# Attention block times SiLU of a GEGLU layer: output weights, last scalings, w_down pieces and first gate sums moved in the order

## The chip, the cores and the metric

The kernel runs on one core of one Trainium2 chip. The time is device microseconds (us) of one execution; the time of a kernel is the median over its runs. Engine names are those of the profile: PE is TensorE, PEld its weight loads, DVE VectorE, ACT ScalarE, POOL GpSimd, SP SyncE, which here only starts DMAs.

## The reference

```python
x  = A_x                                   # 1 x 2048 x 576
xn = layernorm(x)
qkv = xn @ wqkv                            # 32 heads of 18
p  = softmax(q k^T * 18**-0.5);  s = (p v, heads joined) @ wo
g  = silu((gelu_tanh(xn @ w_gate) * (xn @ w_up)) @ w_down)    # inner width 4608
out = x + s * g                            # float32
```

## The kernel before

**Arithmetic.** Products that need float32 accuracy are made of three matmuls: each operand is split into a high part (rounded copy) and a low part (value minus high part), and high x high, high x low and low x high are summed. The splits have names: `wh`, `wl` for the gate and up weights, `ah`, `al` for the GEGLU activations, `T` (both parts of w_down), `woh`, `wol` for the output weights, `oh`, `ol` for the attention result.

**Stages.** A first stage normalises x, transposes it and computes q, k, v into scratch in HBM. Then come 144 *sections*, n = 0 to 143. The tokens are cut into NF = 4 blocks b of 512, the inner width into 18 rounds r of two halves g, and a section multiplies one block by one 128-wide slice of w_gate and w_up: 27 pairs of matmuls, line 412. Its PSUM goes under the tag `f`, or at the end alternately `ring`, a ring of three buffers. Sections 11 to 138 carry the attention between their pairs: scores `pe`, maxima `pm`, values `acc`. Two sections make a *down product* down(b, r): seven products of 42 matmuls in all (line 523) in a Strassen-like scheme with seven accumulators M[0..6]. ScalarE copies them into M in the first round of a block (line 525), VectorE adds them later (line 527).

**Gate sums.** When a block is done, its M are combined into four quarters (`COMBINED`, line 544: four pairs p, q of in-place sums) and stored as `ys` (line 550, `QUARTERS` m = 6, 4, 1, 5). The next block's first down product overwrites M, so it waits for that. `combine_at(i, ...)` hooks a sum ahead of pair i of the next section; `gates` does it for the section after it. Block 0's sums are shared by VectorE (p) and GpSimd (q).

**The end.** The last five sections, 139 to 143, are made by `last_section`. Between them stand the last three down products, `last_down(0..2)`, and 16 output *steps*. `step` n projects 128 tokens (`project`, 28 matmuls, line 1032), multiplies by the gate and adds x (`multiply`), splits the attention result of step n + 2 and loads `ys` and x for later steps. Up to twelve of these stand before the last block's M is ready. `load_wo` and `split_wo` bring the output weights: ScalarE makes woh (line 993), GpSimd wol (line 995), in the buffers that later hold x and ys. The last two attention units (`rest`) are scaled by the reciprocals of their sums: `load_scale` (`on`, `od`), `scale` on GpSimd (lines 704 to 707), `store_scale` (13 small stores, lines 716 to 722). `load_scale` uses the same SBUF (`rawd`, `tsum`) that later holds more x (`xxs`). A down product reads w_down as four pieces of T, each a DMA from the scratch `ts` (`t_piece`, line 468).

**Order.** TensorE's order is written out. On the other compute engines a scheduler places instructions during the sections, within marked ones' program order; from the last five sections on, theirs is written out too. SyncE works through its DMAs in order: one that waits for a landing, for a free buffer or for data holds back all behind it.

Of the kernel before, what the change touches and what calls it, by code (L numbers as in the profile page):

```python
# [30 lines left out]
NU = NQ * NB  # L31
# [24 lines left out]
PIECES = ((0, 3, 7), (0, 0, 3), (1, 3, 7), (1, 0, 3))  # L56
# [25 lines left out]
def kernel(ctx: ExitStack, tc: tile.TileContext, x, wqkv, wo, w_gate, w_up, w_down, out):  # L82
    nc = tc.nc
# [84 lines left out]
    with tc.tile_pool(name="pro", bufs=1) as pro, tc.tile_pool(name="pps", bufs=1, space=PSUM) as pps:  # L168
# [34 lines left out]
        def load_x(b):  # L203
            keep = tc.keep_in_program_order if b == 1 else lambda i: i
            xr = []
            for j in range(4):
                xx = pro.tile([P, D + HR], F32, name="xx", bufs=4)
                keep(nc.sync.dma_start(xx[:, 0:D], x[b * TB + j * P:b * TB + (j + 1) * P, :]))
                xr.append(xx)
            return xr  # L210
# [254 lines left out]
    def t_piece(r, k, store=False):  # L465
        i, a, b = PIECES[k]
        t, d = f(FF["T"])[:, i, a:b].rearrange("p m d -> p (m d)"), ts[r][:, (7 * i + a) * DC:(7 * i + b) * DC]
        nc.sync.dma_start(*((d, t) if store else (t, d)))
# [45 lines left out]
    def down(b, r, then={}):  # L514
        if b == 0 and r < PLAIN:
            return down_plain()
        (ah, al), T, M = FF["A"], FF["T"], FF["M"]
        for m, (i, k) in PRODUCTS:
            py = ring("py")
            for t in range(2):  # L520
                tt = slice(t * P, (t + 1) * P)
                for n, (h, w) in enumerate(((ah, 0), (ah, 1), (al, 0))):
                    nc.tensor.matmul(py[:, t, 0:DC], h[:, i, tt], T[:, w, k], start=n == 0, stop=n == 2)  # L523
            if r == 0:
                nc.scalar.activation(M[:, m], py[:, :, 0:DC], AF.Copy)
            else:
                nc.vector.tensor_tensor(M[:, m], py[:, :, 0:DC], M[:, m], op=ALU.add)  # L527
            for eng, to, op, by in then.get(m, ()):
                eng.tensor_tensor(M[:, to], M[:, to], M[:, by], op=op)
        if r == NR - 1 and b < NB - 1:  # L530
            FF["gates"].append(b)
            if b == 0:
                combine_at(14, nc.vector, *COMBINED[0])
            else:
                for k in range(4):
                    combine_at(6 * k + 6, nc.gpsimd, *COMBINED[k])

    def combine_at(i, eng, p, q):
        FF["hooks"].setdefault(i, []).append(lambda: (combine(eng, *p), combine(nc.gpsimd, *q)))

    def combine(eng, to, op, by):

        M = FF["M"]
        tc.keep_in_program_order(eng.tensor_tensor(M[:, to], M[:, to], M[:, by], op=op))

    def store_gates(b):

        for i, c, m in QUARTERS:
            rows = slice(b * TB + TH * i, b * TB + TH * i + TH)
            nc.sync.dma_start(ys[rows, DC * c:DC * c + DC].rearrange("(t p) d -> p t d", p=P), FF["M"][:, m])  # L550

    def gates():

        for b in FF["gates"]:
            if b == 0:
                for i, k in ((2, 1), (8, 2), (13, 3)):
                    combine_at(i, nc.vector, *COMBINED[k])
                FF["hooks"].setdefault(20, []).append(lambda b=b: store_gates(b))
            else:
                store_gates(b)  # L560
        FF["gates"] = []
# [139 lines left out]
    def scale(u, i):  # L701

        o, d = (t[:, i, 0:TB] for t in SC)
        nc.gpsimd.tensor_tensor(o, o, d, op=ALU.mult)
        if u % NQ == NQ - 1:
            nc.gpsimd.tensor_scalar(d.bitcast(F32R), o, split_rows, 1.0, op0=ALU.mult, op1=ALU.mult)
            nc.gpsimd.tensor_tensor(o, o, d, op=SUB)

    def store_scale(u, i):

        j, g = divmod(u, NQ)
        o, d = (t[:, i, 0:TB] for t in SC)
        for a in range(QD):
            row, p = (QD * g + a) * DH, 32 * a + 1
            if row + DH <= R0:
                nc.sync.dma_start(on[j][row:row + DH, :], o[p:p + DH])
                continue
            k = max(0, R0 - row)
            if k:
                nc.sync.dma_start(on[j][row:R0, :], o[p:p + k])  # L720
            for t, to in ((d, row + k), (o, row + k + HR)):
                nc.sync.dma_start(on[j][to:to + DH - k, :], t[p + k:p + DH])
# [248 lines left out]
    with tc.tile_pool(name="epi", bufs=1, reuse_waits="tile") as epi:  # L971
# [2 lines left out]
        YY = [epi.tile([P, D], F32, name=f"yy{i}") for i in range(4)]  # L974
        OP = {}
        groups = [(b, j) for b in range(NB) for j in range(TB // P)]
        rest, pieces = list(range(scaled, NU)), []
        pool, vec, act = nc.gpsimd, nc.vector, nc.scalar
        n = 0

# [2 lines left out]
        def load_wo():  # L983
            for i, t in enumerate(RAW[:KT]):
                nc.sync.dma_start(t, wo[i * P:(i + 1) * P, :])
            for a in range(2):
                nc.sync.dma_start(RAW[KT][HR * a:HR * a + HR], wo[R0:D, :])
# [13 lines left out]
        def load_y(k):  # L1001
            if k < len(groups) and groups[k][0] < NB - 1:
                nc.sync.dma_start(YY[k % len(YY)], ys[rows(k), :])
# [5 lines left out]
        def split_o(k):  # L1009
            if k < len(groups):  # L1010
                b, j = groups[k]
                oh, ol = OP[k] = [epi.tile([P, KT, P], F32R, name=m, bufs=c) for m, c in (("oh", 3), ("ol", 2))]
                raw = f(KA)[:, OTS[b]:OTS[b] + KT, j * P:(j + 1) * P]
                act.activation(oh, raw, AF.Copy)
                vec.tensor_tensor(ol, raw, f(oh), op=SUB)
# [33 lines left out]
        def step():  # L1049
            nonlocal n  # L1050
            po = project(n)
            multiply(n, po)
            split_o(n + 2)
            b, j = groups[n]
            if b < 2 and j == TB // P - 1:
                load_o(b + 2)
            for t in pieces[:2]:
                t()
            del pieces[:2]
            load_y(n + len(YY))  # L1060
            load_x(n + len(XX))
            n += 1

        def load_raw(n):
            FF["raw"][n] = load_gu(n % (NR * G))

        def last_section(tag):

            n = FF["n"]
            FF["n"] += 1  # L1070
            g = n % G
            pairs, pg, pu = gate_up(tag)
            hooks, FF["hooks"] = FF["hooks"], {}
            nxt = FF["raw"].pop(n + 1, None)
            if nxt:
                split_gu(nxt, 0)
                split_gu(nxt, 1)
            for t in spread(pairs, (), 1, hooks):
                t()
            if nxt:  # L1080
                split_gu(nxt, 2)
            FF["w"] = nxt
            h = ffn.tile([P, 3 + 3 * g, TH], F32, name=f"h{g}", bufs=2 - g)
            t1 = h[:, 0:2].rearrange("p a t -> p (a t)")

            def gelu():
                act.activation(t1, pg, AF.Square)
                vec.scalar_tensor_tensor(t1, t1, 1.0 / GC, pg, op0=ADD, op1=ALU.mult)
                act.activation(t1, t1, AF.Tanh, scale=GC * GS)
                vec.scalar_tensor_tensor(t1, t1, 1.0, pg, op0=ADD, op1=ALU.mult)  # L1090
                vec.tensor_tensor(t1, t1, pu, op=ALU.mult)

            return h, gelu

        def last_down(k, then={}):
            r = NR - 3 + k
            down(NB - 1, r, then)
            if r + 1 < NR:
                pieces.extend(lambda i=i: t_piece(r + 1, i) for i in range(len(PIECES)))

        ctx.enter_context(tc.manual_schedule(engines={mybir.EngineType.Activation, mybir.EngineType.DVE, mybir.EngineType.Pool}))
        FF["down"].clear()
        first = FF["n"]
        load_raw(first + 2)
        h, gelu = last_section("f")
        todo.pop("rec")[0]()
        for i, u in enumerate(rest):
            load_scale(u, i)
        load_wo()
        for k in range(2):  # L1110
            load_y(k)
        load_raw(first + 3)
        gelu()
        sums_a(1, h, vec)
# [1 line left out]
        split_o(0)  # L1116
        h, gelu = last_section("ring")
        gelu()
        for i, u in enumerate(rest):
            scale(u, i)  # L1120
            store_scale(u, i)
        h1, gelu = last_section("f")
        last_down(0)
        split_wo()
        for k in range(3):
            load_x(k)
        for k in range(2, 4):
            load_y(k)
        split_o(1)
        gelu()  # L1130
        sums_a(0, h, pool)
        cut_a(0, h, pool, pool)
        sums_a(1, h1, pool)
        cut_a(1, h1, pool, pool)
        load_raw(first + 4)
        for m in ("rawd", "tsum"):
            t = ffn.tile([P, 2, D], F32, name="xxs", tag=m)
            XX.extend((t[:, 0], t[:, 1]))
        for t in pieces:
            t()  # L1140
        del pieces[:]
        for k in range(3, len(XX)):
            load_x(k)
        for k in range(3):
            step()
# [57 lines left out]
```

## Time and profile before

| | us |
|---|---|
| median of 3 runs | 2601.88 (2599.99 to 2603.06) |
| profiled execution, its own time | 2600.66 |
| its span, first to last instruction | 2598.9 |
| PE busy | 2553.1 (98% of the span) |
| DVE busy | 2083.8 (80%) |
| POOL busy | 1642.1 (63%) |
| ACT busy | 1465.4 (56%) |

The granted clock of TensorE was 0.994 on the mean. Times in a row of the profile count from the span's start. A wait is put down to the event that ended it.

### The profile page before, as it was taken

To read this page: it belongs to the slowest core of one execution; us is meant where nothing else is said; L and a number is where in the kernel's file an instruction comes from. 1 tells how busy PE (TensorE), PEld (TensorE's weight loads), DVE (VectorE), ACT (ScalarE), POOL (GpSimd) and SP (SyncE) were. 2 spreads that over 40 slices of the span, in tenths; PEclk is the share of its full clock that TensorE was granted. 3 is DMA by queue.
4 is the path that set the end of the run, shared out by engine and by line. 5 is a ranking of instruction groups with operands and counts; after the bars stand their busy time and mean duration, and the time that the engine had idled before them with its cause. 6 is when DMAs were issued, how large, how long until landed. Compare 5 with 4: busy or idle time off the path is not lost.

```text
span 2598.9 us, 52905 instructions
## 1 busy us (share of the span) xinstructions
PE 2553.1 (98%) x20548; PEld 1846.2 (71%) x20548; DVE 2083.8 (80%) x2360; ACT 1465.4 (56%) x1772; POOL 1642.1 (63%) x1710
## 2 busy tenths in 40 slices
PE   9999999999999999999999999999999999999987
PEld 8887766666666776666666667766666777667777
DVE  5325888888887888888887988888887988886455
ACT  3224366666666655555566666656566665566511
POOL 3105588888888856666667666666657666666661
PEclk9999999999999999999999999999999999999988
DMA  8855455555575566666786676666677666665673
GB/s 262 270 181 138 108 166 156 165 161 161 166 211 149 165 159 158 167 165 161 172 196 181 168 166 165 166 169 170 169 172 206 169 166 166 154 173 151 186 218 132
DMA packets 410465, 447.47 MB, mean 172 GB/s; under 512 B 107108, under 2 KB 286820, under 8 KB 410216
## 3 DMA queue, kind: packets, MB, share of 16 engines
q1 hardware_dynamic: 410216, 444.09, 64.6%
q8 instruction: 164, 2.69, 0.4%
q14 instruction: 85, 0.70, 0.1%
HBM read 347.59 MB, written 96.38 MB: 171 GB/s over the span
## 4 chain that ended last, share of the span: by engine, by line
PE 92%; POOL 2%; DMA 2%; DVE 1%; issue 1%; ACT 1%; SPq 0%; POOLq 0%; DVEq 0%; ACTq 0%
PE pg L412 21%; PE acc L874 17%; PE py L523 14%; PE pu L412 11%; PE pe L857 9%; PE pm L805 9%; PE po L189 7%; PE po L1032 2%; PE py L510 1%; DMA raw<-in_B_w_up_dram 1%; DVE mx L807 0%; DMA od<-rT 0%; PE pt L250 0%; DMA T<-ts 0%; POOL wl L112 0%
## 5 line engine op out<-in xcount | busy, mean ns | idle before, releaser
L858 ACT ACTIVATE pT<-pe 128x1024 f32<-128x1024 f32 x1024 | 1047.2, 1027 | 577.9 <-PE pe L857 544.6
L807 DVE TENSOR_REDUCE mx<-pm 128x2 f32<-128x1024 f32 x1024 | 1221.3, 1224 | 181.8 <-PE pm L805 165.7
L412 PE MATMUL pg<-xd,wh 64*128 64x512 f32 x2538 | 925.5, 396 | 1.9 <-ACT t L425 1.9
L412 PE MATMUL pu<-xd,wh 64*128 64x512 f32 x2538 | 925.7, 396 | 1.6 <-DVE t L426 1.6
L412 PEld LDWEIGHTS pg<-xd,wh 64*128 64x128 f32 x2538 | 467.9, 184 | 114.8 <-issue 56.9
L412 PE MATMUL pg<-xd,wl 64*128 64x512 f32 x1269 | 496.1, 391 | 1.1 <-POOL wl L117 1.1
L412 PE MATMUL pu<-xd,wl 64*128 64x512 f32 x1269 | 496.0, 391 | 0.0
L412 PEld LDWEIGHTS pu<-xd,wh 64*128 64x128 f32 x2538 | 468.2, 184 | 27.6 <-DVE t L426 2.9
L874 PE MATMUL acc<-pT,VS 128*32 128x512 f32 x4096 | 466.0, 595 | 0.0
L110 POOL TENSOR_SCALAR wh<-raw 128x384 fp32r<-128x384 f32 x402 | 215.5, 539 | 385.1 <-PE pu L412 262.7
L112 POOL TENSOR_TENSOR wl<-raw,wh 128x384 fp32r<-128x384 f32 x402 | 416.9, 1039 | 27.7
L805 PE MATMUL pm<-KA,QT 64*128 64x512 f32 x2048 | 414.1, 394 | 4.6 <-ACT pT L858 2.8
L857 PE MATMUL pe<-QT,KA 64*128 64x512 f32 x2048 | 411.2, 392 | 3.4 <-DVE mx L807 2.4
L523 PE MATMUL py<-T,ah 128*128 128x288 f32 x1876 | 385.0, 301 | 13.2 <-DMA T<-ts 9.9
L527 DVE TENSOR_TENSOR M<-py,M 128x576 f32<-128x576 f32 x448 | 339.0, 757 | 42.5 <-PE py L523 28.8
L523 PEld LDWEIGHTS py<-T,ah 128*128 128x128 f32 x1876 | 302.0, 190 | 68.0 <-issue 54.0
L441 POOL TENSOR_TENSOR al<-h,ah 128x512 fp32r<-128x512 f32 (+1 forms) x143 | 296.7, 2075 | 65.4 <-ACT ah L438 53.8
L874 PEld LDWEIGHTS acc<-pT,VS 128*32 128x32 f32 x4096 | 120.2, 110 | 276.6 <-issue 229.6
L523 PE MATMUL py<-T,al 128*128 128x288 f32 x938 | 277.8, 296 | 0.0
L857 PEld LDWEIGHTS pe<-QT,KA 64*128 64x128 f32 x2048 | 193.1, 184 | 115.0 <-DVE mx L807 28.6
L412 PEld LDWEIGHTS pg<-xd,wl 64*128 64x128 f32 x1269 | 234.1, 184 | 32.8 <-POOL wl L117 2.0
L412 PEld LDWEIGHTS pu<-xd,wl 64*128 64x128 f32 x1269 | 234.1, 184 | 13.2
(169 smaller groups left out, 2921.3 us busy)
## 6 DMA issues: line engine op xcount, KB each, us to landing
T<-ts SPq DMA_DIRECT2D x98, 576.0 KB
KA<-qk SPq DMA_DIRECT2D x768, 72.0 KB
T<-ts SPq DMA_DIRECT2D x98, 432.0 KB
raw<-in_B_w_gate_dram SPq DMA_DIRECT2D x144, 288.0 KB
raw<-in_B_w_up_dram SPq DMA_DIRECT2D x144, 288.0 KB
ts<-T SPq DMA_DIRECT2D x36, 576.0 KB
VS<-vs SPq DMA_DIRECT2D x128, 152.0 KB
qk<-t SPq DMA_DIRECT2D x72, 256.0 KB
```

The costliest lines, as they stand in the source:

```text
L110: first = nc.gpsimd.tensor_scalar(hi, raw, 1.0, 1.0, op0=ALU.mult, op1=ALU.mult)
L112: keep(nc.gpsimd.tensor_tensor(lo, raw, f(hi), op=ALU.subtract))
L189: nc.tensor.matmul(o, st, m, start=(i == 0), stop=(i == len(terms) - 1))
L412: nc.tensor.matmul(o, w[1 + wp][k][rr, c, :], xd[k][xp][rr, c, :], start=(i == 0), stop=(i == len(terms) - 1))
L441: keep(two.tensor_tensor(lo, raw, f(hi), op=ALU.subtract))
L523: nc.tensor.matmul(py[:, t, 0:DC], h[:, i, tt], T[:, w, k], start=n == 0, stop=n == 2)
L527: nc.vector.tensor_tensor(M[:, m], py[:, :, 0:DC], M[:, m], op=ALU.add)
L805: nc.tensor.matmul(pm[:, a], QS[u, r][rr, t * P:(t + 1) * P], KS[(u * NA + c) % KB][r][rr, :], start=True, stop=True)
L807: return nc.vector.tensor_reduce(MX[u][:, 2 * r:2 * r + 2, t, c], pm, axis=AX.X, op=ALU.max)
L857: nc.tensor.matmul(pe[:, a], KS[(u * NA + c) % KB][r][rr, t * P:(t + 1) * P], QS[u, r][rr, :], start=True, stop=True)
L858: nc.scalar.activation(PT[u, kt][:, 2 * r:2 * r + 2, :], pe, AF.Exp, scale=SCALE)
L874: nc.tensor.matmul(ACC[u][32 * a:32 * a + 32, :], VS[(u * NA + c) % VB][:, v:v + 32], pt[:, a, :], start=first, stop=last, skip_group_chec ...
```

## The change

There are four edits.

1. *Gate sums.* GpSimd's halves q of block 0's sums are hooked at pairs 6, 12, 18 and 24 of the section right behind the block, all four there; VectorE's first half p stays at pair 14 and its others at 2, 8 and 13 of the section behind that. The quarters m = 1 and 5 are stored at the end of the first of these sections, 4 and 6 at pair 19 of the second. Before, only the first q was in the first section, and all four stores came at pair 20. For blocks 1 and 2 only the order of p and q within a pair is swapped.
2. *Output weights.* `load_wo` stands ahead of section 139 in place of behind `load_scale`; `split_wo`, three x loads and two ys loads stand behind section 140 in place of behind section 141 and down(0).
3. *Last units.* `scale` stands behind section 141 and down(0), `store_scale` behind the load of the last raw weights. Before, both were behind section 140.
4. *w_down.* `last_down` issues its four T pieces at once. Before, the steps behind it issued two each, or they stood behind the load of the last raw weights. x is loaded one step less ahead.

```diff
@@ down, combine_at, store_gates, gates
+            for k, (p, q) in enumerate(COMBINED):
+                combine_at(6 * k + 6, nc.gpsimd, q)
+                if b > 0:
+                    combine_at(6 * k + 6, nc.gpsimd, p)
             if b == 0:
-                combine_at(14, nc.vector, *COMBINED[0])
-            else:
-                for k in range(4):
-                    combine_at(6 * k + 6, nc.gpsimd, *COMBINED[k])
+                combine_at(14, nc.vector, COMBINED[0][0])
...
-    def combine_at(i, eng, p, q):
-        FF["hooks"].setdefault(i, []).append(lambda: (combine(eng, *p), combine(nc.gpsimd, *q)))
+    def combine_at(i, eng, what):
+        FF["hooks"].setdefault(i, []).append(lambda: combine(eng, *what))
...
-    def store_gates(b):
+    def store_gates(b, some=range(7)):
         for i, c, m in QUARTERS:
+            if m not in some:
+                continue
...
             if b == 0:
+                store_gates(b, (1, 5))
                 for i, k in ((2, 1), (8, 2), (13, 3)):
-                    combine_at(i, nc.vector, *COMBINED[k])
-                FF["hooks"].setdefault(20, []).append(lambda b=b: store_gates(b))
+                    combine_at(i, nc.vector, COMBINED[k][0])
+                FF["hooks"].setdefault(19, []).append(lambda b=b: store_gates(b, (4, 6)))
@@ step
-            for t in pieces[:2]:
-                t()
-            del pieces[:2]
             load_y(n + len(YY))
-            load_x(n + len(XX))
+            load_x(n + len(XX) - 1)
@@ last_down
             if r + 1 < NR:
-                pieces.extend(lambda i=i: t_piece(r + 1, i) for i in range(len(PIECES)))
+                for i in range(len(PIECES)):
+                    t_piece(r + 1, i)
@@ the end
         load_raw(first + 2)
+        load_wo()
         h, gelu = last_section("f")
         todo.pop("rec")[0]()
+        for k in range(2):
+            load_y(k)
         for i, u in enumerate(rest):
             load_scale(u, i)
-        load_wo()
-        for k in range(2):
-            load_y(k)
...
         gelu()
-        for i, u in enumerate(rest):
-            scale(u, i)
-            store_scale(u, i)
-        h1, gelu = last_section("f")
-        last_down(0)
         split_wo()
         for k in range(3):
             load_x(k)
         for k in range(2, 4):
             load_y(k)
+        h1, gelu = last_section("f")
+        last_down(0)
         split_o(1)
         gelu()
+        for i, u in enumerate(rest):
+            scale(u, i)
...
         load_raw(first + 4)
+        for i, u in enumerate(rest):
+            store_scale(u, i)
...
-        for t in pieces:
-            t()
-        del pieces[:]
-        for k in range(3, len(XX)):
+        for k in range(3, len(XX) - 1):
             load_x(k)
```

GpSimd before, from the last low part of section 141's weights to the first sum of section 140's activations (`on`, `od` are the last units, `wh`, `wl` the weights of section 142):

```order
L112 TENSOR_TENSOR wl<-raw,wh 128x384
L704 TENSOR_TENSOR on<-on,od 128x512 x2
L706 TENSOR_SCALAR od<-on,split_rows 128x512
L707 TENSOR_TENSOR on<-on,od 128x512
L110 TENSOR_SCALAR wh<-raw 128x384
L112 TENSOR_TENSOR wl<-raw,wh 128x384
L110 TENSOR_SCALAR wh<-raw 128x384
L112 TENSOR_TENSOR wl<-raw,wh 128x384
L110 TENSOR_SCALAR wh<-raw 128x384
L112 TENSOR_TENSOR wl<-raw,wh 128x384
L991 MEMSET wol 64x576
L995 TENSOR_TENSOR wol<-xx_31043,woh 128x576
```

GpSimd now, from the same place (line numbers are four higher):

```order
L112 TENSOR_TENSOR wl<-raw,wh 128x384
L995 MEMSET wol 64x576
L999 TENSOR_TENSOR wol<-xx_31043,woh 128x576
L999 TENSOR_TENSOR wol<-xx_31044,woh 128x576
L999 TENSOR_TENSOR wol<-xx_31045,woh 128x576
L999 TENSOR_TENSOR wol<-yy_31048,woh 128x576
L999 TENSOR_TENSOR wol<-yy_31049,woh 64x576
L110 TENSOR_SCALAR wh<-raw 128x384
L112 TENSOR_TENSOR wl<-raw,wh 128x384
L110 TENSOR_SCALAR wh<-raw 128x384
L112 TENSOR_TENSOR wl<-raw,wh 128x384
L110 TENSOR_SCALAR wh<-raw 128x384
```

The five wol have gone from behind the scaling and the splits of section 142 to ahead of both; the scaling now follows these splits.

SyncE now, from the last piece of T for down(1) over the raw weights of section 143 to ys for step 4 (`on_72` is the last block's scaled result in HBM):

```order
L468 DMA T<-ts 128x864
L130 DMA raw<-in_B_w_gate_dram 64x9x128
L130 DMA raw<-in_B_w_up_dram 64x9x128
L720 DMA on_72<-on 18x512 x4
L724 DMA on_72<-on 8x512
...
L726 DMA on_72<-od 18x512
L726 DMA on_72<-on 18x512
L1011 DMA xxs<-in_A_x_dram 128x576 x3
L1051 DMA out_dram<-xx_31043 128x576
L1007 DMA yy_31046<-ys 128x576
```

The stores of the scaled units, which stood ahead of the x loads of the first steps, now stand behind the raw weights of section 143 and ahead of the loads into their own buffers (`xxs`), the first output and ys for step 4.

ScalarE behind down(1,0), before and then now (`M<-py` are the copies of the seven products, `T` the next w_down, `pT` the attention's exponentials):

```order
L525 ACTIVATE M<-py 128x576 x6
L483 ACTIVATE T<-tsum 128x1152
L525 ACTIVATE M<-py 128x576
L485 ACTIVATE T<-tsum 128x288
L486 ACTIVATE T<-rawd 128x576
L858 ACTIVATE pT<-pe 128x1024 x8
```

```order
L525 ACTIVATE M<-py 128x576 x5
L483 ACTIVATE T<-tsum 128x1152
L485 ACTIVATE T<-tsum 128x288
L486 ACTIVATE T<-rawd 128x576
L862 ACTIVATE pT<-pe 128x1024
L525 ACTIVATE M<-py 128x576 x2
L862 ACTIVATE pT<-pe 128x1024 x7
```

Two of the seven copies have moved behind the three T copies and the first pT.

More of the change, by code (lines that the diff above doesn't have):

```diff
@@ L976 @@
         groups = [(b, j) for b in range(NB) for j in range(TB // P)]
-        rest, pieces = list(range(scaled, NU)), []
+        rest = list(range(scaled, NU))
         pool, vec, act = nc.gpsimd, nc.vector, nc.scalar
```

## The prediction

> **What bounds the kernel now.** I read the page first, then the waits of the end, then TensorE's own rows there, then the engines and transfers that it waited for. The page:
>
> ```profile
> PE 2553.1 (98%) x20548; PEld 1846.2 (71%) x20548; DVE 2083.8 (80%) x2360; ACT 1465.4 (56%) x1772; POOL 1642.1 (63%) x1710
> PE   9999999999999999999999999999999999999987
> ```
>
> TensorE is full in every slice but the last two, so a change is worth what it takes out of TensorE's gaps. The waits from 2440 us to 2600 us name the gaps of the end (total, times, longest):
>
> ```profile
> PE po L1032 <- POOL wol L995: 10.5, 5, 9.4
> PE py L523 <- DMA T<-ts: 9.9, 2, 9.0
> ```
>
> TensorE's rows around them (start, duration; the wait ahead in brackets), first of the output step 0, then of the last down product:
>
> ```profile
> 2480.25 0.29 PE L1032 MATMUL po<-woh,oh 128*128 128x288 f32 x1
> 2489.94 0.61 PE L1032 MATMUL po<-wol,oh 128*128 128x288 f32 x1 [9.39 <-POOL wol L995]
> 2498.67 0.42 PE L1032 MATMUL po<-woh,KA 128*128 128x288 f32 x1
> 2498.91 0.32 PE L1032 MATMUL po<-wol,KA 128*128 128x288 f32 x1
> 2499.06 0.29 PE L1032 MATMUL po<-woh,oh 128*128 128x288 f32 x1
> 2548.57 0.37 PE L523 MATMUL py<-T,ah 128*128 128x288 f32 x1 [0.89 <-DMA T<-ts]
> 2557.91 0.61 PE L523 MATMUL py<-T,ah 128*128 128x288 f32 x1 [8.97 <-DMA T<-ts]
> 2566.06 0.30 PE L1032 MATMUL po<-woh,oh 128*128 128x288 f32 x1
> ```
>
> After each gap the matmuls start 0.24 us apart (2498.67 to 2498.91), later about 0.135. A gap therefore costs its length and a stretch at half rate. What the same work takes without a gap stands in the chain of waits (start, length):
>
> ```profile
> 2450.26 5.79 PE py L523 x42
> 2506.76 6.37 PE pgu L412 x54
> 2513.13 11.32 PE po L1032 x84
> 2549.51 8.36 DMA T<-ts
> ```
>
> Three steps of 28 matmuls take 11.32 us, so one takes 3.77 and one matmul 0.135. Step 0 took 2499.06 - 2480.25 = 18.81 us, so 15.0 are lost. The last down product waited 0.89 + 8.97 = 9.9 us and then ran from 2557.91 to 2566.06, 8.15 us against 5.79, so 2.4 more are lost. The end holds 15.0 + 9.9 + 2.4 = 27.3 us that no work needs.
>
> **The output weights ahead of the first stall.** GpSimd's rows show why wol was late (in brackets the idle time before):
>
> ```profile
> 2465.13 1.02 POOL L112 TENSOR_TENSOR wl<-raw,wh 128x384 fp32r<-128x384 f32 x1
> 2473.92 1.29 POOL L704 TENSOR_TENSOR on<-on,od 128x512 f32<-128x512 f32 x1 [2.56 <-DMA od<-rT]
> 2483.09 0.51 POOL L110 TENSOR_SCALAR wh<-raw 128x384 fp32r<-128x384 f32 x1 [5.68 <-DMA on<-on]
> 2486.79 0.99 POOL L112 TENSOR_TENSOR wl<-raw,wh 128x384 fp32r<-128x384 f32 x1
> 2488.49 4.11 POOL L995 TENSOR_TENSOR wol<-xx,woh 128x576 fp32r<-128x576 f32 x3
> 2492.56 2.77 POOL L995 TENSOR_TENSOR wol<-yy,woh 128x576 fp32r<-128x576 f32 x2
> 2495.29 0.72 POOL L447 TENSOR_TENSOR h<-h 128x256 f32<-128x256 f32 x1
> 2502.55 3.28 POOL L441 TENSOR_TENSOR al<-h,ah 128x1280 fp32r<-128x1280 f32 x1
> ```
>
> The five wol stood behind the scaling, which waited for od, and behind the splits of section 142, which began only at 2483.09. After the change they stand behind the splits of 141 alone, which end at 2466.15. They then wait only for ScalarE's woh:
>
> ```profile
> 2472.54 0.63 ACT L1089 ACTIVATE h<-h 128x512 f32<-128x512 f32 x1 [2.84 <-DVE h L1088]
> 2474.73 2.14 ACT L993 ACTIVATE woh<-xx 128x576 fp32r<-128x576 f32 x3 [1.56 <-DMA xx<-in_A_wo_dram]
> ```
>
> On SyncE's queue the wo loads now stand ahead of three T pieces, the store of the reciprocals and the scale loads, so the 1.56 us that woh waited for them should go, and woh follows the gelu at 2473.2 at 0.71 us a piece. The first wol can start at 2473.9 and five at 1.38 us end near 2480.8. Step 0 needs the first wol at 2480.4 and the fifth some 1.5 us later. The cover is thin, 1 us, but it is there: I take the whole 15.0, and each us that woh comes later costs under one.
>
> The Trainium skill, "TensorE: Matmul & The Clock Gate", Part 1, says that an idle TensorE drops to half clock and comes back after about 3.4 us of sustained work. In the last down product the half rate lasted longer: 2.4 us lost at 0.24 - 0.135 a matmul are 23 matmuls or 5.5 us. By the skill's window it would be an estimated 14 matmuls, 1.5 us lost for 2.4, and the sum 26.4; the measured row decides.
>
> **What is late next.** Everything behind step 0 comes 15.0 us sooner: section 142 at 2491.8, down(1) at 2509.5, down(2) at 2532.5. GpSimd: wol to 2480.8, the three splits of 142 (4.7 us from 2483.09 to 2487.78) to 2485.5, the scaling (three products of 1.29 us and a shorter one, 4.6 as an estimate) to 2490.1, sums and cuts of 140 and 141 (2495.29 to 2505.83, 10.5) to 2500.7. Section 142 needs its splits at 2491.8 and down(1) its cuts at 2509.5: 6 and 9 us of room, so both moves cost nothing unless the raw weights of 142 land over 6 us later than that. Scaling goes behind these splits and no more waits for od in front of them.
>
> **w_down asked for at once.** Before, two pieces of T went out per output step and the last pair only at 2549.51, landing 8.36 us later. Now all four follow down(1), which ends near 2515.3, in one group; at the same 8.4 us, doubled because four go together, they land by 2532 at the latest against a need at 2532.5. All 9.9 and 2.4 us go. Room: 0 to 8 us.
>
> **The price: the stores of the scaled units.** These 13 small stores stood from 2476 us on SyncE's queue; now they stand after the scaling and ahead of the x loads into the same buffers (xxs), the first outputs and ys for steps 4 and 5:
>
> ```profile
> 2476.22 2.07 SPq L716 DMA_DIRECT2D on<-on  x4
> 2484.69 0.33 SPq L722 DMA_DIRECT2D on<-on  x1
> ```
>
> They took 2476.22 to 2485.0, 8.8 us, of SyncE's time. From 2490.1 on that ends at 2498.9; three xxs loads, an output and the ys of step 4 follow, landing near 2505. VectorE needs it at the end of step 4, 2491.8 + 6.4 + 7.5 = 2505.7. The trace of before has no such wait, so I bound it: 0 if they land in time, 5 us if od lands twice the 2.56 us late that it cost before, and the scaling and its stores with it. I take 1.5. For the load of the last scaled units ahead of step 10, behind an output on the queue, I take 0.5. The x loads, one step less ahead, still have six steps of 3.77 us, which costs nothing. End: 27.3 - 2.0 = 25.3 us.
>
> **The gate sums of the first block.** They stood in the section ahead of down(1,0), and the copies of the next products into M waited:
>
> ```profile
> 788.87 1.40 POOL L544 TENSOR_TENSOR M<-M 128x576 f32<-128x576 f32 x1
> 790.30 0.65 ACT L525 ACTIVATE M<-py 128x576 f32<-128x576 f32 x1 [3.49 <-POOL M L544]
> 785.01 0.53 PE L523 MATMUL py<-T,ah 128*128 128x288 f32 x2
> 791.01 0.53 PE L523 MATMUL py<-T,ah 128*128 128x288 f32 x2 [2.57 <-ACT M L525]
> 795.61 0.33 PE L523 MATMUL py<-T,al 128*128 128x288 f32 x1
> 796.53 1.16 ACT L483 ACTIVATE T<-tsum 128x1152 fp32r<-128x1152 f32 x1
> 799.02 2.85 ACT L858 ACTIVATE pT<-pe 128x1024 f32<-128x1024 f32 x3
> 768.90 1.28 POOL L450 TENSOR_TENSOR h<-h,h 128x512 f32<-128x512 f32 x1 [2.78 <-DVE h L429]
> ```
>
> TensorE took 795.74 - 785.01 = 10.7 us for 5.79, so 4.9 are lost. Three GpSimd sums of 1.4 us, 4.3 in all, move one section up, into its idle 2.78; the cuts there end 1.5 us later, still ahead of down(1,0) at 785.01, where no wait for them shows. New is ScalarE's order behind down(1,0): the copies of two of the seven products come after the T copies (1.16, two shorter ones) and one pT (2.85 / 3 = 0.95), about 3.3 us, and hold two of three PSUM buffers for that time. That new wait lies between 0 and 3.3; most of it meets a TensorE that needs buffers for scores, so I take 2.4. Gain 4.9 - 2.4 = 2.5, bounds 0 to 4.9, and -1 if the maxima behind slip too.
>
> **Sum.** The profiled execution took 2600.66 us (span 2598.9): 2600.66 - 25.3 - 2.5 = 2572.9. The median of the three runs is 2601.88, 1.2 above that one, so the forecast is 2574. Alone it spans 2567 (27.3 and 4.9 gained, and the 3 us by which the runs differ) to 2580 (stores 5 us late, gate sums worth nothing).
>
> **Rivals.** *Transfers bound the end.* The queue of 2453 to 2558 us, then stretches of it (TensorE, its loads, VectorE, ScalarE, GpSimd, clock, share, GB/s):
>
> ```profile
> q1 hardware_dynamic: 13078, 23.45, 74.0%
> 2477.00:2480.00 3.00, 3.00 (x25) 3.00 (x24) 2.82 (x5) 2.38 (x4) 0.40 (x1) 1.00 1.12 195
> 2480.00:2492.00 12.00, 2.34 (x11) 1.75 (x9) 3.75 (x6) 1.15 (x2) 8.53 (x10) 0.72 0.25 66
> 2501.00:2510.00 9.00, 9.00 (x71) 8.16 (x71) 7.80 (x7) 1.26 (x2) 8.83 (x5) 1.00 1.03 385
> ```
>
> These 23.45 MB kept the engines busy for 0.74 x 105 = 77.7 us. They must now land by about 2541, in 88 us, a share of 0.88. The gaps to fill are there (0.25 from 2480 to 2492), but SyncE asks in order and may stand before a wait while they are empty. At a share of 0.80 the last lands at 2453 + 97 = 2550, 9 us late: 2583. At the old 0.74 it is 2558, 17 late: 2591. For it speaks the thin row of the stores, against it that T now stands early in the queue. Chance 0.22. The Trainium skill, "DMA: Bandwidth & Descriptors", Specifications, gives about 358 GB/s as a core's limit at HBM; by that the 23.45 MB would take an estimated 66 us and fit with ease. The trace has 385 in one stretch, above it, and 302 on average while busy, so the rows are the stricter measure, and I follow them.
>
> *The gate sums return their gain.* ScalarE's late copies push scores and maxima by the full 3.3 us and more: 2574 + 2.5 to 5, about 2577. Chance 0.08.
>
> *It does not do what it says.* woh comes late, say behind a wo load that waits for its buffers, and half of the first stall stays: 2574 + 7.5 = 2581.5. Against it, xx and yy are fresh buffers then. Chance 0.04.
>
> *Slower.* The packed transfers run at the rate that raw weights, od and wo ran at together, 195 GB/s at full share (the row at 2477). 23.45 MB then take 120 us and the last lands at 2573, 15 us after today's 2557.9: with the half-rate product back and the gate gain, 2600.66 + 15 - 2.5 + 1.2 = 2614. It decides for slower below 23.45 MB / 107 us = 219 GB/s. Against it stands 385 GB/s in the row at 2501, and 302 on average. Chance 0.06.
>
> **How the numbers follow.** The forecast has 0.60. From 2567 to 2587 the range holds it, the gate rival, the half stall and the milder half of the transfers, about 0.83. The measurement can tell 0.2%, 5 us: every case but the last lies over 8 us below 2601.88. Of the last's 0.06, 0.02 lies about no change; of the rest, 0.02 lies as near to either side. So faster 0.92, same 0.03, slower 0.05.
>
> **What would show it.** Right: wol at about 2474 to 2481 on GpSimd, no wait of po for wol, T of the last product in one group near 2515, its wait gone, down(2) done near 2540, and the tail of 2598.9 - 2566.06 = 32.8 us unchanged; around 785 no wait of M for GpSimd, and a new one for pT or M. Wrong: waits of VectorE for yy<-ys before down(1), of TensorE for T or KA near 2530 to 2545, or wol still behind od.

## The result and the profile after

The changed kernel takes 2575.94 us (median of 4 runs, 2575.34 to 2577.57), the kernel before 2601.89 us (4 runs); the ratio is 0.9902, 95% interval 0.9885 to 0.9919. Forecast were 2574 us, between 2567 and 2587. The profiled execution has a span of 2573.6 us, 25.3 less than before. The page of the changed kernel; TensorE is now full in 39 slices of 40:

```profile
PE 2546.1 (99%) x20548; PEld 1838.3 (71%) x20548; DVE 2089.8 (81%) x2360; ACT 1464.9 (57%) x1772; POOL 1640.2 (64%) x1710
PE   9999999999999999999999999999999999999998
```

TensorE's waits of the end, 2440 us to 2600 us. Both of before are gone (10.5 for wol, 9.9 for T). The wait of 1.6 for `ol` was there before; what has come is 1.4 for VectorE's multiply `yy` and short ones:

```profile
PE po L1036 <- DVE ol L1019: 1.9, 2, 1.6
PE py L523 <- DVE yy L1045: 1.4, 1, 1.4
PE py L523 <- DVE M L527: 0.8, 2, 0.5
```

GpSimd at the end: wol at 2472.18 to 2479.18, then a wait for the raw weights of section 142, the scaling, and the cuts to 2504.77:

```profile
2472.18 4.22 POOL L999 TENSOR_TENSOR wol<-xx,woh 128x576 fp32r<-128x576 f32 x3 [6.01 <-issue]
2476.37 2.81 POOL L999 TENSOR_TENSOR wol<-yy,woh 128x576 fp32r<-128x576 f32 x2
2483.32 0.52 POOL L110 TENSOR_SCALAR wh<-raw 128x384 fp32r<-128x384 f32 x1 [4.14 <-DMA raw<-in_B_w_up_dram]
2488.87 3.00 POOL L708 TENSOR_TENSOR on<-on,od 128x512 f32<-128x512 f32 x2
2501.82 2.95 POOL L441 TENSOR_TENSOR al<-h,ah 128x1280 fp32r<-128x1280 f32 x1
```

SyncE: ys for step 4 leaves at 2501.37, behind the 13 stores; T for the last down product in one group at 2525.18. TensorE takes that product up at 2534.36 without a wait and ends it at 2540.75:

```profile
2497.83 0.32 SPq L726 DMA_DIRECT2D on<-on  x1
2499.54 1.31 SPq L1011 DMA_DIRECT2D xxs<-in_A_x_dram  x3
2501.37 0.43 SPq L1007 DMA_DIRECT2D yy<-ys  x1
2525.18 1.81 SPq L468 DMA_DIRECT2D T<-ts  x4
```

The gate sums, 755 us to 812 us. TensorE's waits there are these; those of M for GpSimd (3.3 us of TensorE's time before) are gone, the maxima's are not:

```profile
PE pe L861 <- DVE mx L811: 3.7, 4, 1.9
PE pm L809 <- ACT pT L862: 2.1, 1, 2.1
PE pe L861 <- ACT M L525: 0.3, 1, 0.3
```

Before, the waits for the maxima in the same stretch were these:

```profile
PE pe L857 <- DVE mx L807: 1.8, 4, 0.7
```

The order on TensorE is the same in both kernels, but for neighbouring matmuls that change places (those of `pg` and `pu` above all), so the start of each matmul can be set against its twin. The difference is called the lead here. The changed kernel is 0.1 us ahead at 755 us, 2.1 us behind at the end of the section ahead of down(1,0), 2.7 ahead at the end of down(1,0), and 0.2 us ahead 6 us later. The lead is 0.6 at 2440, 15.7 after step 0, 15.9 at 2500, 13.2 after the waits in down(1), and 25.3 after the last down product and at the end. The end thus gave 24.7 us and the gate sums next to nothing.

### The profile page after: what moved, and what is told of

Read it like the earlier page. It is cut to its first block, busy times and chain, and to the rows that moved or that the text cites. A ratio compares the mean times of both kernels' runs of the same rounds, so it can differ in the third digit from the quotient of the medians.

```text
span 2573.6 us, 52904 instructions
## 1 busy us (share of the span) xinstructions
PE 2546.1 (99%) x20548; PEld 1838.3 (71%) x20548; DVE 2089.8 (81%) x2360; ACT 1464.9 (57%) x1772; POOL 1640.2 (64%) x1710
```

## Experiments

Each chip's own runs of the kernel before gave 2599 to 2600.2 us; ratios are to those.

**The two parts apart.** `end_only`:

```diff
-            for k, (p, q) in enumerate(COMBINED):
-                combine_at(6 * k + 6, nc.gpsimd, q)
...
+            if b == 0:
+                combine_at(14, nc.vector, *COMBINED[0])
+            else:
+                for k in range(4):
+                    combine_at(6 * k + 6, nc.gpsimd, *COMBINED[k])
...
-                store_gates(b, (1, 5))
```

> The edits of the end alone; the gate sums of the first block stand as before the change. The prediction priced the gate sums at 2.5 us, so this would be 2575.9 + 2.5 = 2578.4 us. The theory after the result: the gate sums gained 4.9 us in down(1,0) but lost about 1.9 us in the section ahead of it, where VectorE's sums into M last until GpSimd's instruction beside them ends, and about 2.2 us behind it, where the maxima wait for ScalarE; the net is 0.2 to 0.9 us, so 2576.1 to 2576.8 us.

Measured: 2575.28 us, ratio 0.9909 (0.9895 to 0.9922), 25.0 us under the 2600.24 of that chip. `gate_only` is the reverse, the kernel before with the change's gate sums alone:

> The gate sums alone; the end stands as before the change. By the prediction's price 2601.9 - 2.5 = 2599.4 us. By the theory after the result 2601.0 to 2601.7 us, with TensorE free of waits in down(1,0), 3 to 4 us of waits for the maxima (VectorE) in the section ahead of it and a wait of 2 us for pT behind it.

Measured: 2601.51 us (11 runs, 2598.0 to 2606.3), ratio 1.0008 (1.0000 to 1.0017). The end alone makes the whole gain. The gate sums give nothing, or cost up to 0.17%; neither price of mine, 2.5 or 0.2 to 0.9 us, was low enough.

**Where the gate sums lose.** First the sums split over two sections, with all four stores at pair 19 of the second, `gate_split`:

```diff
             for k, (p, q) in enumerate(COMBINED):
-                combine_at(6 * k + 6, nc.gpsimd, q)
+                if b > 0 or k < 2:
+                    combine_at(6 * k + 6, nc.gpsimd, q)
...
                 for i, k in ((2, 1), (8, 2), (13, 3)):
                     combine_at(i, nc.vector, COMBINED[k][0])
+                    if k < 3:
+                        combine_at(i, nc.gpsimd, COMBINED[k + 1][1])
```

> The change, but with only two of GpSimd's four sums in the section behind the block and the other two in the next one behind the long cut (al, 1280 columns), and all four stores at pair 19 there. If VectorE's sums are drawn out because GpSimd's long cut was pushed beside them, this gives back 1.5 to 2 us there, and with the copies of M ahead of the T copies again another 1 us behind: 2572.9 to 2574.4 us, VectorE's third sum back from 2.49 to about 1.1 us. If the place of the cut does not matter, that part is unchanged, and the later sums and stores cost up to 3 us in down(1,0): 2575.9 to 2579 us.

Measured: 2574.8 us, ratio 0.9904 (0.9890 to 0.9917), not to be told from the change. VectorE's last sum (the third of its section, the fourth in all) fell to 1.14 us as expected, but its first one, a section earlier, took 3.94 us in this execution, and TensorE waited 3.3 us there. The same showed in `gelu_first` (below), whose code is that of the change in this part. Its VectorE and GpSimd rows, and the matmul that waited (start, duration):

```profile
760.64 4.17 DVE L545 TENSOR_TENSOR M<-M 128x576 f32<-128x576 f32 x1
764.73 3.54 DVE L811 TENSOR_REDUCE mx<-pm 128x2 f32<-128x1024 f32 x3
760.04 0.83 POOL L493 TENSOR_TENSOR T<-tsum,T 128x288 fp32r<-128x288 f32 x1
760.81 1.45 POOL L494 TENSOR_TENSOR T<-rawd,T 128x576 fp32r<-128x576 f32 x1
762.19 1.43 POOL L545 TENSOR_TENSOR M<-M 128x576 f32<-128x576 f32 x1
763.56 0.64 POOL L440 TENSOR_SCALAR ah<-h 128x512 fp32r<-128x512 f32 x1
764.28 1.64 POOL L441 TENSOR_TENSOR al<-h,ah 128x512 fp32r<-128x512 f32 x1
766.00 0.50 PE L861 MATMUL pe<-QT,KA 64*128 64x512 f32 x2 [3.52 <-DVE mx L811]
```

VectorE's sum reads two tensors of SBUF. It began beside GpSimd's work and ended at 764.81, 0.6 us after GpSimd's `ah` at 764.20; three instructions of GpSimd that followed each other without a gap had gone first. In the changed kernel's own profile the first sum came through (0.79 us) and the last did not: 777.35 to 779.84, 0.6 us after GpSimd's long cut ended at 779.22:

```profile
776.27 2.95 POOL L441 TENSOR_TENSOR al<-h,ah 128x1280 fp32r<-128x1280 f32 x1
777.35 2.49 DVE L545 TENSOR_TENSOR M<-M 128x576 f32<-128x576 f32 x1
```

The Trainium skill, "SBUF — State Buffer", section "SBUF: two separate sides", calls VectorE's and GpSimd's shared port pair an exclusive lock held for the whole instruction, also against VectorE instructions with two SBUF inputs when GpSimd's instruction reads SBUF. The rows agree, and add that the loser can miss several turns in a row. VectorE's first sum started 0.66 us behind GpSimd's T part of 0.83 us in the profile of the change and came through; in that of `gelu_first` it started 0.60 us behind the same part and did not. So less than 0.1 us lies between both outcomes, and executions of the same code differ: 0.2 us of TensorE's time at this place in the profile of the change, 3.5 in that of `gelu_first`.

Then ScalarE's copies alone, `gate_keep`:

```diff
-                nc.scalar.activation(M[:, m], py[:, :, 0:DC], AF.Copy)
+                tc.keep_in_program_order(nc.scalar.activation(M[:, m], py[:, :, 0:DC], AF.Copy))
```

> The change, with ScalarE's seven copies into M held ahead of the T copies behind down(1,0), and nothing else. If the late copies cost what the wait of 2.1 us for pT shows, it goes: 2573.5 to 2574.2 us. If the held VectorE ahead of down(1,0) is the larger part, the waits of pe for the maxima there stay at 3.7 us and over.

Measured: 2573.08 us, ratio 0.9896 (0.9882 to 0.9911), not to be told from the change. The wait for pT fell from 2.1 to 1.3 us, in an execution whose first VectorE sum took 3.64 us and kept TensorE waiting for 3.0. Both causes together, `gate_late`: the copies kept as here, and GpSimd's sums split as in `gate_split` but with the first two at pairs 20 and 24:

```diff
+                if b > 0 or k < 2:
+                    combine_at(6 * k + 6 if b > 0 else 4 * k + 20, nc.gpsimd, q)
```

> The change, with GpSimd's four sums at other places: two at pairs 20 and 24 of the section behind the block, where GpSimd sat idle, and two in the next one behind the long cut; the four stores together at pair 19; ScalarE's seven copies into M held ahead of the T copies. Theory of the held VectorE: its first sum and its third are no longer beside GpSimd's, so the waits of pe for the maxima fall back to about 1.8 us as before the change, down(1,0) waits 1 us or less, and the wait for pT behind it goes: 2575.9 - 2 to 4 = 2572 to 2574 us. Rival: the gate sums are worth nothing wherever they stand, because sums later in the section are late for down(1,0) again: 2575 to 2577 us.

Measured: 2568.4 us (2567.4 to 2568.9), ratio 0.9883 (0.9868 to 0.9898), more than I expected. TensorE's waits, and VectorE's first and last sum, in its profile:

```profile
PE pe L863 <- DVE mx L813: 1.9, 4, 0.7
PE pe L863 <- ACT pT L864: 0.4, 1, 0.4
PE pm L811 <- DVE mx L813: 0.2, 1, 0.2
760.17 1.32 DVE L546 TENSOR_TENSOR M<-M 128x576 f32<-128x576 f32 x1
776.12 1.13 DVE L546 TENSOR_TENSOR M<-M 128x576 f32<-128x576 f32 x1
```

The waits for the maxima are about those of before, down(1,0) has none, and pT's is 0.4 us: set against the change matmul by matmul, it gains 2.0 us ahead of down(1,0) and 5.6 in all from 755 us to behind it. Part of that is no wait: in the profile of the change TensorE ran at half its clock from 798.1 to 801.5 us, behind the wait for pT, and started 16 matmuls in that time, against 28 in the 3.4 us from 802.0 on. In `gate_late` the granted clock is 1.00 there. The row of the change (TensorE, its loads, VectorE, ScalarE, GpSimd, clock, share, GB/s):

```profile
798.10:801.50 3.40, 3.40 (x19) 3.40 (x17) 1.85 (x3) 2.02 (x2) 3.32 (x4) 0.51 0.09 30
```

`gate_late` is 30.6 us under its chip's 2599.02, the end alone gave 25.0: well placed, and with ScalarE's copies kept ahead, the gate sums are worth about 5.6 us, though the intervals of the two ratios just touch. That `gate_split` differs ahead of down(1,0) by the places of the first two sums alone, and waits 4.5 us for the maxima there against 1.9, puts that loss on the place.

**The two stalls of the end apart.** `t_only` is the kernel before with the T pieces of the fourth edit alone (x is loaded as early as before):

```diff
-                pieces.extend(lambda i=i: t_piece(r + 1, i) for i in range(len(PIECES)))
+                for i in range(len(PIECES)):
+                    t_piece(r + 1, i)
```

> The kernel before with the four T pieces of each of the last down products issued at once, and nothing else. The prediction's terms: the wait of 9.9 us and the 2.4 us at half rate go, 12.3 in all: 2601.9 - 12.3 = 2589.6 us. Rival, transfers bound the end: the loads of ys and x behind the T pieces come later and VectorE and TensorE wait for them, a gain of 5 to 8 us: 2594 to 2597 us.

Measured: 2587.46 us, ratio 0.9955 (0.9939 to 0.9972), 11.6 us under its chip's 2599.02, against 12.3 foretold. `no_t` is the change without those pieces at once:

> The change without the T pieces at once: two of them follow each output step, as before. If the two stalls of the end are independent, the second one comes back in full: 2575.9 + 12.3 = 2588.2 us. If the early output weights alone made room for T (everything asked for earlier), less comes back, 2578 to 2584 us; if transfers bind, more than 12.3, 2590 us and over.

Measured: 2591.34 us, ratio 0.9972 (0.9962 to 0.9981): only 7.7 us gained, so inside the change the T pieces are worth about 16 us by the spans of the two profiles (2589.8 and 2573.6) and 18 by the two gains (7.7 and 26.0, each against its own chip's runs of before). TensorE's waits of its end:

```profile
PE py L523 <- DMA T<-ts: 10.4, 2, 8.9
PE py L523 <- DVE yy L1045: 3.6, 2, 2.6
PE po L1036 <- DVE ol L1019: 2.1, 2, 1.6
```

The old wait for T is back in full, and the waits for VectorE's `yy` grow from 1.4 to 3.6 us: T for down(1) now stood behind the 13 stores, leaving at 2498.84, and the x and ys loads behind T, ys for step 4 at 2503.21. So the transfers do crowd there, as the first rival had it, when T isn't asked for early.

**The new wait in down(1).** `gelu_first` puts VectorE's GELU of section 142 ahead of step 3:

```diff
+        gelu()
         for k in range(3):
             step()
-            if k == 0:
-                gelu()
```

> The change, but with VectorE's and ScalarE's GELU of section 142 ahead of output step 3 in place of behind it. Theory of the held VectorE: the wait of 1.4 us ahead of the last product of down(1) comes from ol of step 5, which lasted 3.38 us beside GpSimd's cut, with the GELU and the multiply of step 4 behind it; with the GELU earlier most of it goes: 2574.4 to 2575.2 us. The prediction's theory: VectorE waited for ys behind the 13 stores; then nothing changes, 2575.9 us.

Measured: 2576.29 us, ratio 0.9910 (0.9897 to 0.9924). No gain. I had put the wait on `ol` of step 5, which ran 2501.94 to 2505.32 beside the cut of 2501.82; with the GELU out from behind it, `ol` was held again (2.65 us), VectorE then waits for ys (1.48 and 1.31 us) and TensorE 1.0. `add1_gelu` adds step 1's sum on VectorE:

```diff
-            (pool if k % 2 and k < SHARED else vec).tensor_tensor(xx, xx, t, op=ADD)
+            (pool if k % 2 and 1 < k < SHARED else vec).tensor_tensor(xx, xx, t, op=ADD)
```

> The change with the GELU of section 142 ahead of output step 3, and with the addition of x in step 1 on VectorE in place of GpSimd. Theory: the ys load of step 5 reuses the buffer of step 1 and stands on SyncE behind the output of step 1, both of which wait for GpSimd's addition at 2504.7 to 2506.6 us, behind its cuts; VectorE is free for it near 2488, so the load goes out near 2502, and TensorE's 1.0 to 1.4 us ahead of the last product of down(1) go: 2574.3 to 2575.0 us. By the prediction's theory the 13 stores hold these loads, and they still do: 2575.5 to 2576.5 us, with VectorE still waiting for ys ahead of step 5's multiply.

Measured: 2575.83 us, ratio 0.9912 (0.9897 to 0.9926). My second theory fell too: VectorE waits 4.0 us, for ys of step 4, which left at 2501.94 behind the stores, and TensorE 1.2 us for VectorE's `yy`:

```profile
2501.94 0.43 SPq L1007 DMA_DIRECT2D yy<-ys  x1
2506.84 0.75 DVE L1045 SCALAR_TENSOR_TENSOR yy<-yy,po 128x576 f32<-128x576 f32 x1 [4.01 <-DMA yy<-ys]
```

That is the prediction's price. `stores_late` takes it away, with the addition on VectorE but the GELU where the change has it (`step(False)` is a step without its x load):

```diff
+        step(False)
         for i, u in enumerate(rest):
             store_scale(u, i)
...
-        for k in range(3):
+        for k in range(2):
             step()
```

> The change, with the 13 stores of the scaled units and the x loads behind them moved behind output step 0, so that the output of step 0 and the ys load of step 4 go out ahead of the stores, and with the addition of x in step 1 on VectorE. The prediction's theory, that the stores hold the ys load of step 4: TensorE's wait ahead of the last product of down(1) falls from 1.0 to 2.0 us to under 0.5 and VectorE no longer waits for ys there: 2574.0 to 2575.0 us against 2575.9. Rival, VectorE held by GpSimd alone makes that wait: it stays, 2575.5 to 2576.5 us.

Measured: 2574.51 us, ratio 0.9907 (0.9890 to 0.9923). The ys load leaves at 2489.56, VectorE no longer waits for it, and TensorE's wait falls from 1.4 to 0.2 us:

```profile
2489.56 0.42 SPq L1007 DMA_DIRECT2D yy<-ys  x1
PE py L523 <- DVE yy L1045: 0.2, 1, 0.2
```

In the whole time 1.4 us lies within the interval; the wait itself is shown by the profile. `ol` took 1.24 us in this execution, so a held `ol` is gone from it too. Two other profiles tell the causes apart. In that of the change VectorE waits for no ys between 2501.27 and 2511.94: there the held `ol` (3.38 us) is what made the wait. In that of `end_only`, whose end is the same, `ol` took 0.68 us, VectorE waits 1.15 us for ys of step 5, and TensorE's wait is 1.2 all the same:

```profile
2509.86 0.76 DVE L1041 SCALAR_TENSOR_TENSOR yy<-yy,po 128x576 f32<-128x576 f32 x1 [1.15 <-DMA yy<-ys]
2510.76 0.50 PE L523 MATMUL py<-T,ah 128*128 128x288 f32 x2 [1.23 <-POOL wh L110]
```

The view names GpSimd's wh, but the matmul starts 0.14 us behind the end of that multiply, as it does in the profile of the change (0.15). So each cause is enough without the other.

**All together**, `best3`, `gate_late` with the edits of `stores_late`:

> GpSimd's sums two and two and ScalarE's copies as in the run that gave 2568.4 us, with the stores behind step 0 and step 1's addition on VectorE. If the gains add, 2567.0 to 2568.0 us; if TensorE's wait ahead of down(1)'s last product has another cause, 2568.4 us again.

Measured: 2568.24 us (2568.14 to 2568.42), ratio 0.9878 (0.9864 to 0.9893): the fastest, 31.7 us under its chip's 2599.97 where the change gave 26.0, and not to be told from `gate_late`. Its interval lies wholly below that of `end_only` (0.9895 to 0.9922); the `stores_late` edits alone gave 0.9907, so most of the difference is that of the well placed gate sums. The wait of 2.0 us in down(1) that `gate_late` still had is gone; elsewhere this execution ran later, by 0.7 us ahead of 755 and by 1.2 between 1640 and 1650.

## Why the prediction was right, and the step that was not

- **Output weights, 15.0 us:** measured 15.1 (lead 15.7 after step 0, 0.6 ahead of it). wol ran 1.7 us sooner than reckoned.
- **T at once, 9.9 and 2.4 us:** measured 12.1 from lead to lead (13.2 to 25.3) with a new wait of 0.5 in it, and 11.6 alone. The half rate behind the wait was 2.4 by the row. The lead grows by 9.2 at the wait's end and by 1.9 more to the product's end; without the new 0.5 it would be 2.4, as in the row.
- **What is late next:** the raw weights of 142 kept GpSimd waiting to 2483.32, and the scaling's four instructions were busy for 5.9 us, against 4.6 reckoned; the cuts ended at 2504.8 in place of 2500.7. The room of 9 us took both in. T went out 10 us later than reckoned, at 2525.18, and still came in time for 2534.36. Had it taken the 8.4 us of the last pair of before, an estimated 0.8 us were left, near the lower end of the prediction's 0 to 8.
- **The stores, 2.0 us in all:** the lead falls by 2.7 (15.9 to 13.2), and there is the 0.5 above. The place, down(1) by way of VectorE's multiply, was right. The way to it was right only in part: in the profile of the change the held `ol` caused the wait, which the prediction did not have, and late ys did in those of `end_only` and `add1_gelu`. That the size came near is luck to that extent. The load ahead of step 10, priced at 0.5, cost nothing.
- **The gate sums, 2.5 us: the step that failed.** The sizes of its two priced terms were right: 4.9 in down(1,0) (measured 4.8) and 2.4 behind it (2.5). In the second there is luck: TensorE's waits for ScalarE there grew only from 1.0 to 2.4 us, and the rest falls in the stretch at half clock from 798.1 on, which the term did not have. What the step left out was a third: I had only asked whether the cuts that the sums delay come in time for down(1,0), and let VectorE run beside GpSimd at no cost. It cost 2.2 us in the profile of the change; by the waits for the maxima (1.8 us before) 2.4 in that of `gate_keep` and 5.0 in that of `gelu_first`. That takes the gain away. The end's -25.3 stood, at 25.0 in `end_only`, so the time missed by 1.9 us, about what the gate sums failed to give.
- **The rivals.** Transfers did not bind: from 2453 to 2541 the queue moved 22.99 MB at a share of 0.849, where 0.88 was asked for, and TensorE waited for none of it in the profile of the change. The rival on the gate sums came true in its size by another mechanism than the one named.

```profile
q1 hardware_dynamic: 12847, 22.99, 84.9%
```

## What to carry to other kernels

Take a stall out by asking what stands ahead of the late instruction on its own in-order engine or queue; when two stalls sit on one queue, price them together, since the T pieces here are worth 12 us alone and 16 to 18 with the other edits. When work is moved to GpSimd, look not only whether it comes in time: look which VectorE instructions with two SBUF inputs run at that moment and who waits for VectorE. Place it where GpSimd has gaps and VectorE reads PSUM; here that was about 5 us.

## What the runs showed of the hardware

A VectorE instruction of 0.7 to 1.3 us that reads two SBUF tensors lasted 2.49, 3.38, 3.64, 3.94 and 4.17 us beside GpSimd, and ended each time 0.5 to 0.6 us behind the end of a GpSimd instruction. VectorE's maxima, which read PSUM, kept 1.2 us each throughout. GpSimd's own instruction can be the one that waits: the T part beside VectorE's first sum in the profile of the change took 1.97 us, against 1.44 before. These races make the first of the same gate sums cost 0.2, 3.0 or 3.5 us of TensorE's time in the profiles of the change, `gate_keep` and `gelu_first`.

Some waits of TensorE cost more than their length. Behind the 2.1 us for pT the granted clock was 0.51 for 3.4 us in the profile of the change, and behind the 3.5 us for the maxima it was 0.50 for 3.4 us in that of `gelu_first`; in the kernel before it was 0.50 from 792.3 to 795.7, inside down(1,0). Behind 3.3 us in `gate_split` and 3.0 us in `gate_keep` it stayed at 1.00, so the length of a wait alone does not tell.
